# Layer norm's epsilon and wrap-around copy move from GpSimd to VectorE, the first q pieces are split for two token blocks, and two planner constants change

## The chip, the cores and the metric

One core of a Trainium2 chip runs the whole kernel. The metric is the device time in microseconds of one execution. Five engines work side by side, each through its own program in order: TensorE (PE: matmuls, and PEld: its weight loads), VectorE (DVE), ScalarE (ACT), GpSimd (POOL), and SyncE (SP), which here only issues DMA transfers. Engines wait for each other through semaphores.

## What is computed

One layer with two branches on the same normalised input: sliding-window attention with 32 heads of 18 and a gated feed-forward. Cut to what matters:

```python
xn = (x - mean(x)) / sqrt(var(x) + 1e-5)          # x: 2048 tokens x 576
q, k, v = split(xn @ wqkv)                        # wqkv: 576 x 1728
p = softmax(where(0 <= i - j < 256, q @ k.T * 18**-0.5, -1e9))
s = (p @ v).reshape(2048, 576) @ wo
h = sigmoid(xn @ w_gate) * (xn @ w_up)            # 576 x 4608 each
out = x + s * silu(h @ w_down)                    # 4608 x 576
```

## The kernel before

**Tiles and stages.** The 2048 tokens are four chunks of 512, a chunk four blocks of 128 tokens. Chunk c goes through layer norm (`build_ln`), the projections (`build_qkv`, 12 of them, q, k and v of each block), attention (`build_attn`), the output projection (`build_wo`), gate and up of the feed-forward with the down projection behind it (`build_ffn`). Gate and up fill TensorE; the scores and P*V of the same chunk are interleaved with them in small units.

**Layer norm of a block** (lines 424 to 441), in names used below: two statistics over half a row each, `bn1` and `bn2` (VectorE); the aggregate `ag` to mean and variance (VectorE); `ve`, the variance plus epsilon, one number per token (GpSimd, L431); `rstd`, that number to the power of -0.5 (GpSimd, L433); `apply`, subtract the mean and multiply by rstd over 576 columns (VectorE, L437) into a row of 640; and `wrap`, which fills columns 576 to 639 of that row with the normalised first 64 columns (GpSimd, L441: the same formula on 64 columns of x). The wrapped row serves the transposed layout: nine slices of 64 features, each present on both halves of the partitions.

**Into the transposed layout.** In chunk 0 TensorE transposes the row in nine pieces of 128 columns, the first four (`XT_CUT`) behind `apply` and the other five behind `wrap` (L462, `tr`); ScalarE copies each group out of the accumulator into `xn` (L472, `xe`). In chunks 1 to 3 two DMA transposes a block do that (`xt`), which wait for `apply` and `wrap`, and for the feed-forward of the chunk before to be done with `xn`.

**Projections.** `project` (L486) makes q, k or v of one block out of nine slices for two halves of the columns, 18 matmuls. For q of block 0 of chunk 0 alone they are two operations: the first four slices, which need only the first ScalarE copy and the first two of the four weight loads, and the rest. The order of the projections of chunk 0 is chosen by the planner; q and k of chunk 0 then go through DMA transposes (`qkt`) into `qkp`, from which the scores read.

**What sets the order.** The kernel is written as a list of operations with an engine, an estimated duration, dependencies and a priority. `schedule` plays them through: at each step an engine takes the operation with the smallest (earliest start + 40 ns x priority), the start being the planned time at which its dependencies are done, and for a DMA that plus a `slack`. The result is a fixed program for each engine; on the chip each operation waits on semaphores alone, so planned times decide the order and nothing else. In chunk 0 the layer norm of block i has the priority `LN_STEP * (i - 4)` on VectorE, TensorE and ScalarE, -12, -9, -6, -3; `ve` and `rstd` have 0. `XT0_SLACK` is the slack of `qkt` in chunk 0: so many ns after the planned landing the scores may be planned. Weights are issued on SP's queue, in the order of priorities: x, wqkv, then gate and up in groups of three tiles of 128 columns.

Of the kernel before, what the change touches and what calls it, by code (L numbers as in the profile page):

```python
# [5 lines left out]
ALU = mybir.AluOpType  # L6

S = 2048
D = 576
# [15 lines left out]
DP = NKT * P  # L25
EPS = 1e-5
# [53 lines left out]
XT0_ISSUE_NS = 1500.0  # L80
OC_SLACK = 3000.0
LATE_SLACK = 5000.0
LN_STEP = 3
EZ = 2
XT_CUT = 4
SC_GATE = 0
PV_PRIO = (2, 3)
PC_PRIO = 1
# [11 lines left out]
X0_FACTOR = 1.7  # L100
XT_BYTES = 1.2
XT0_BYTES = 1.5
XT0_SLACK = 1200.0
W0_FACTOR = 1.5
DMA_LAT_NS = 1600.0
DMA_BYTES_PER_NS = 320.0
# [2 lines left out]
def mm_ns(n):  # L109
    return max(28.0, n / 2.4 + 2.5)  # L110


def act_ns(n):
    return n / 1.2 + 80.0
# [72 lines left out]
class Builder:  # L187
# [16 lines left out]
    def op(self, eng, occ, fn, name, deps=(), prio=3, **kw):  # L204
        o = Op(eng, occ, fn, name, deps, prio, **kw)
        o.cidx = len(self.ops)
        self.ops.append(o)
        return o
# [199 lines left out]
    def build_ln(self, c):  # L408
        op = self.op
        pr = 0 if c == 0 else 2  # L410
        _, dxn = self.r_xn.take()
        self.op_xn = [[] for _ in range(QPC)]
        for i in range(QPC):
            st = c * QPC + i
            if c == 0:
                pr = LN_STEP * (i - QPC)
            ring, buf = (self.r_xf, self.xf) if c == 0 and i >= NXR else (self.r_xr, self.xr)
            sx, dx = ring.take()
            xs = buf[:, sx, :]
            o_x = self.dma(xs, self.x[st * P:(st + 1) * P, :], (X0_FACTOR if c == 0 and i > 1 else 1.0) * P * D * 2, f"x{st}",  # L420
                           ("x", i if c == 0 else sx), deps=dx + ([self.op_f1[(c - 1, 6 + 3 * i)]] if c > 0 else []),
                           prio=X_PRIO[i] if c == 0 else 4, slack=X0_SLACK if c == 0 else LATE_SLACK)
            sb_, db_ = self.r_bn.take()
            b1 = op("DVE", 360, lambda e, sb_=sb_, xs=xs: e.bn_stats(self.bnst[:, sb_, 0, :], xs[:, 0:288]),  # L424
                    f"bn1:{st}", deps=[o_x] + db_, prio=pr)
            b2 = op("DVE", 360, lambda e, sb_=sb_, xs=xs: e.bn_stats(self.bnst[:, sb_, 1, :], xs[:, 288:576]),
                    f"bn2:{st}", deps=[o_x] + db_, prio=pr)
            ag = op("DVE", 120, lambda e, st=st, sb_=sb_: e.bn_aggr(self.mv[:, st, :], self.bnst[:, sb_, :, :]),
                    f"ag:{st}", deps=[b1, b2], prio=pr)
            self.r_bn.release(sb_, ag)  # L430
            ve = op("POOL", 100, lambda e, st=st: e.tensor_scalar(self.veps[:, st, :], self.mv[:, st, 1:2], EPS,  # L431
                                                                 None, ALU.add), f"ve:{st}", deps=[ag], prio=0)
            rs = op("POOL", 560, lambda e, st=st: e.tensor_tensor(self.rstd[:, st, :], self.veps[:, st, :],  # L433
                                                                 self.neghalf[:, :], ALU.pow),
                    f"rstd:{st}", deps=[ve, self.op_negh], prio=0)
            sr, dr = self.r_xnr.take()
            ap = op("DVE", 350, lambda e, st=st, xs=xs, sr=sr: e.tensor_scalar(  # L437
                self.xnr[:, sr, 0:D], xs, self.mv[:, st, 0:1], self.rstd[:, st, :],
                ALU.subtract, ALU.mult), f"apply:{st}", deps=[rs, ag] + dr, prio=pr)
            ring.release(sx, ap)  # L440
            wr = op("POOL", 200, lambda e, st=st, xs=xs, sr=sr: e.tensor_scalar(  # L441
                self.xnr[:, sr, D:DP], xs[:, 0:64], self.mv[:, st, 0:1], self.rstd[:, st, :],
                ALU.subtract, ALU.mult), f"wrap:{st}", deps=[rs, ag] + dr, prio=pr)
            ring.release(sx, wr)
            tok = slice(i * P, (i + 1) * P)
            if c > 0:
                for k, (i0, i1, col) in enumerate(((0, NKT, 0), (NKT, NC, 64))):
                    o = self.dma(self.xn[:, i0:i1, tok], self.xnr[:, sr, col:col + (i1 - i0) * P],
                                 XT_BYTES * (i1 - i0) * P * P * 2, f"xt:{st}.{k}", ("xt", i, k), deps=[wr, ap] + dxn,
                                 prio=-2, issue=XT_ISSUE_NS, transpose=True)  # L450
                    self.r_xnr.release(sr, o)
                    self.op_xn[i].append(o)
                continue
            cols = [k * P for k in range(NKT)] + [64 + k * P for k in range(NC - NKT)]
            for i0, i1, dep in ((0, XT_CUT, ap), (XT_CUT, NC, wr)):
                n = i1 - i0
                ps = Psum((4,), (5,), (6,), (7,), (0,), (1,), (2,), (3,))

                def f_tr(e, sr=sr, ps=ps, i0=i0, i1=i1):
                    b = ps.banks[0] * 1024  # L460
                    for k, col in enumerate(cols[i0:i1]):
                        r = e.transpose(self.psb[:, b + k * P:b + (k + 1) * P], self.xnr[:, sr, col:col + P],  # L462
                                        self.op_[:, NOT - 1, 0:P])
                    return r
                tr = self.pe(n * 58, f_tr, f"tr:{st}", deps=[dep, ap, self.op_ident] + dxn, prio=pr, psum=[ps])
                tr.keep = False
                self.r_xnr.release(sr, tr)

                def f_xe(e, i=i, ps=ps, i0=i0, n=n):
                    b = ps.banks[0] * 1024  # L470
                    src = self.psb[:, b:b + n * P].rearrange("p (k c) -> p k c", k=n)
                    return e.activation(self.xn[:, i0:i0 + n, i * P:(i + 1) * P], src, ACTF.Copy)  # L472
                self.op_xn[i].append(self.rd("ACT", act_ns(n * P), f_xe, f"xe:{st}", deps=[tr], prio=pr, psum=[ps]))
        self.all_xn = [o for l in self.op_xn for o in l]
        if c == 0:
            for o in self.op_ez[EZ:]:
                o.odeps += self.op_xn[-1]

    def project(self, c, i, j, name, deps, after=None):
        ps = Psum((4, 5), (6, 7), (0, 1), (2, 3))  # L480

        def f(e, k0, k1):
            for k in range(k0, k1):
                for hf in range(2):
                    r0 = 64 * hf
                    r = e.matmul(self.bank(ps, HV, hf), self.xn[r0:r0 + 64, k, i * P:(i + 1) * P],  # L486
                                 self.wqkv_sb[r0:r0 + 64, j, k, :], start=(k == 0), stop=(k == NC - 1),
                                 tile_position=(r0, 0))
            return r
        odeps = [after]  # L490
        k0 = 0
        if c == 0 and i == 0 and j == 0:
            k0 = XT_CUT
            odeps = [self.pe(k0 * mm_ns(HV), lambda e: f(e, 0, k0), name + ":0",
                             deps=self.op_xn[i][:1] + self.op_wqkv[j][:2] + deps, prio=1, psum=[ps], mode="r64")]
        o = self.pe((NC - k0) * mm_ns(HV), lambda e: f(e, k0, NC), name, deps=self.op_xn[i] + self.op_wqkv[j] + deps,
                    prio=1, psum=[] if k0 else [ps], mode="r64", odeps=odeps)
        if k0:
            ps.users.append(o)
        self.r_xn.release(0, o)  # L500
        return o, ps
# [20 lines left out]
    def build_qk(self, c, i, j, old):  # L522
# [21 lines left out]
        if c == 0:  # L544
            if j == 0:
# [3 lines left out]
            dm = self.dma(dst, both, 2 * XT0_BYTES * 8 * P * P * 2, f"qkt:{c}:{i}", ("qk", i), deps=[ev, self.op_qe[i]] + old,  # L549
                          prio=0, issue=XT0_ISSUE_NS, transpose=True, slack=XT0_SLACK)  # L550
            if i > 0:
# [285 lines left out]
    def build_ffn(self, c):  # L837
# [67 lines left out]
        for n0, n1 in zip(cuts, cuts[1:]):  # L905
# [69 lines left out]
            prev = o  # L975
            if n0 == SC_GATE and c > 0:
                for l in self.op_sc[c]:
# [339 lines left out]
```

## Time and profile before

| | us |
|---|---|
| median of 3 runs (565.69 to 565.73) | 565.73 |
| the profiled execution | 565.84 |
| its span, first to last instruction | 564.1 |
| TensorE busy in it | 555.5 |
| VectorE busy | 302.9 |
| ScalarE busy | 279.3 |
| GpSimd busy | 44.0 |

A row of the timeline gives the start and the length in us, the engine, the line of the kernel, the operation, what is written and read, the shapes and how many instructions were merged; in brackets stand the idle time ahead of it and what ended that. A row of the stretches gives the length of the stretch and then, for PE, PEld, DVE, ACT and POOL, the busy time and the number of instructions, then TensorE's granted clock, the share of DMA time (it can pass 1, as transfers overlap) and GB/s. A row of the chain of waits gives start, length and what the end of the program hung on at that time. A row of DMA issues gives how many, how large, and the us from the issue to the landing. Matmuls are pipelined, and the end of a matmul row is modelled.

### The profile page before, as it was taken

How to read it: one execution, taken by the hardware profiler on the slowest of the kernel's cores; microseconds unless marked ns; L12 is line 12 of the kernel's file. 1: busy time of each engine (PE TensorE's matmuls, PEld its weight loads, DVE VectorE, ACT ScalarE, POOL GpSimd, SP SyncE). 2: the span in 40 equal slices, each digit the busy share in tenths (PEclk: the TensorE clock that was granted, in tenths of full speed). 3: DMA queues.
4: the chain of work that ended last, by engine and by line, in shares of the span. 5: the costliest groups of instructions: out<-in, count | busy, mean ns of one | idle time of the engine just before them, and what ended most of it. 6: DMA issues, size and time to landing. Idle time of an engine off the chain costs nothing.

```text
span 564.1 us, 17922 instructions
## 1 busy us (share of the span) xinstructions
PE 555.5 (98%) x7831; PEld 287.7 (51%) x7854; DVE 302.9 (54%) x624; ACT 279.3 (50%) x382; POOL 44.0 (8%) x87
## 2 busy tenths in 40 slices
PE   7999999999999999999999999999999999999997
PEld 4644444458544444456754444445665444444554
DVE  5135988722136886772214778666211576776312
ACT  7437777414155847721407575580230856856021
POOL 5000201110000210020000021002000000000100
PEclk9999999999999999999999999999999999999999
DMA  8999978929945766225893566604589365650010
GB/s 200 223 204 181 215 184 218 239 62 135 186 96 132 163 143 158 60 52 87 145 217 73 136 153 136 154 27 68 94 152 189 76 128 128 148 130 24 20 43 23
DMA packets 125900, 73.31 MB, mean 130 GB/s; under 512 B 54654, under 2 KB 125310, under 8 KB 125822
## 3 DMA queue, kind: packets, MB, share of 16 engines
q1 hardware_dynamic: 125822, 72.16, 61.3%
q8 instruction: 62, 1.02, 0.8%
q14 instruction: 16, 0.13, 0.1%
HBM read 55.48 MB, written 2.36 MB: 103 GB/s over the span
## 4 chain that ended last, share of the span: by engine, by line
PE 96%; POOL 1%; issue 1%; DVE 1%; ACT 0%; DMA 0%; DVEq 0%; POOLq 0%
PE ps L874 51%; PE ps L1001 23%; PE ps L486 9%; PE ps L632 5%; PE ps L702 3%; PE ps L795 3%; PE ps L1032 2%; POOL rstd L433 0%; POOL xnr L441 0%; DMA xr<-in_A_x_dram 0%; ACT expr L650 0%; POOL veps L431 0%; PE ps L462 0%; DVE hT L892 0%; DVE bnst L424 0%
## 5 line engine op out<-in xcount | busy, mean ns | idle before, releaser
L874 PE MATMUL ps<-xn,wgs 64*128 64x512 bf16 x2522 | 290.0, 377 | 0.2 <-DVE hT L892 0.2
L874 PEld LDWEIGHTS ps<-xn,wgs 64*128 64x128 bf16 x2522 | 116.4, 94 | 139.8 <-issue 10.3
L650 ACT ACTIVATE expr<-ps 128x1024 bf16<-128x1024 f32 x152 | 149.3, 1023 | 23.5 <-PE ps L632 23.5
L1001 PE MATMUL ps<-wd_sb,hT 128*128 128x64 bf16 (+1 forms) x1057 | 131.1, 284 | 2.1 <-issue 1.3
L888 ACT ACTIVATE tring<-ps 128x512 bf16<-128x512 f32 x144 | 86.2, 599 | 77.5 <-PE ps L874 59.4
L892 DVE SCALAR_TENSOR_TENSOR hT<-tring,ps 128x512 bf16<-128x512 bf16 x144 | 98.3, 683 | 46.3 <-ACT tring L888 23.9
L1001 PEld LDWEIGHTS ps<-wd_sb,hT 128*128 128x128 bf16 x1080 | 68.2, 98 | 65.0 <-issue 1.4
L668 DVE TENSOR_TENSOR expr<-expr,m 128x512 bf16<-128x512 bf16 (+2 forms) x152 | 58.1, 412 | 37.9 <-ACT expr L650 36.8
L1063 ACT ACTIVATE thf<-ps 128x576 bf16<-128x576 f32 (+2 forms) x17 | 10.6, 623 | 133.0 <-PE ps L1001 125.4
L1065 DVE SCALAR_TENSOR_TENSOR thf<-thf,ps 128x576 bf16<-128x576 bf16 (+2 forms) x17 | 12.2, 719 | 109.0 <-ACT thf L1063 108.9
L486 PE MATMUL ps<-wqkv_sb,xn 64*128 64x288 bf16 x864 | 55.0, 283 | 0.0
L486 PEld LDWEIGHTS ps<-wqkv_sb,xn 64*128 64x128 bf16 x864 | 42.7, 94 | 10.4 <-issue 0.5
L632 PEld LDWEIGHTS ps<-qkp 18*64 18x64 bf16 x1472 | 16.4, 103 | 32.8 <-ACT expr L650 18.2
L632 PE MATMUL ps<-qkp 18*64 18x320 bf16 (+4 forms) x1472 | 32.4, 259 | 0.0
L679 POOL COPY qkp<-qkp 128x256 bf16<-128x256 bf16 x24 | 9.8, 409 | 247.4 <-PE ps L632 247.4
L759 DVE STREAM_TRANSPOSE op__63<-pk 128x512 bf16<-128x512 bf16 x32 | 22.5, 702 | 0.3
L702 PEld LDWEIGHTS ps<-expr,vau 64*32 64x32 bf16 x1440 | 17.9, 92 | 7.2 <-issue 5.1
L702 PE MATMUL ps<-expr,vau 64*32 64x320 bf16 (+5 forms) x1440 | 20.7, 253 | 0.0
L1067 DVE TENSOR_TENSOR thf<-thf,sat 128x576 bf16<-128x576 bf16 (+2 forms) x17 | 7.5, 440 | 23.2 <-ACT sat L819 22.9
L795 PE MATMUL ps<-wo_sb,oT 64*128 64x288 bf16 x288 | 18.8, 283 | 0.2 <-issue 0.2
L319 POOL MEMSET pk<- 128x2048 bf16 x4 | 7.2, 1805 | 147.8 <-DVE op__63 L759 147.8
L541 ACT ACTIVATE pk<-ps 128x576 bf16<-128x576 f32 x13 | 8.5, 652 | 15.9 <-PE ps L486 13.6
(63 smaller groups left out, 246.5 us busy)
## 6 DMA issues: line engine op xcount, KB each, us to landing
wgs<-in_B_w_gate_dram SPq DMA_DIRECT2D x47, 240.0 KB, 3.8
wgs<-in_B_w_up_dram SPq DMA_DIRECT2D x47, 240.0 KB, 4.8
wgs<-in_B_w_up_dram SPq DMA_DIRECT2D x47, 192.0 KB, 4.1
wgs<-in_B_w_gate_dram SPq DMA_DIRECT2D x47, 192.0 KB, 4.4
wd_sb<-in_B_w_down_dram SPq DMA_DIRECT2D x9, 576.0 KB, 6.8
xf<-in_A_x_dram SPq DMA_DIRECT2D x18, 144.0 KB, 2.6
out_dram<-xf SPq DMA_DIRECT2D x15, 144.0 KB, 2.0
xr<-in_A_x_dram SPq DMA_DIRECT2D x14, 144.0 KB, 4.9
```

Source lines behind the costliest of these rows:

```text
L486: r = e.matmul(self.bank(ps, HV, hf), self.xn[r0:r0 + 64, k, i * P:(i + 1) * P], self.wqkv_sb[r0:r0 + 64, j, k, :], start=(k == 0), stop=( ...
L632: r = e.matmul(self.ps[64 * half:64 * half + 64, b:b + n * 64], self.qkp[r0:r0 + DH, hg, k0:k0 + 64], self.qkp[r0:r0 + DH, hg, q0 * 64:(q0 ...
L650: return e.activation(self.expr[:, es, 2 * pr:2 * pr + 2, :], src, ACTF.Exp, scale=SM_SCALE)
L668: return e.tensor_tensor(ap, ap, m, ALU.mult)
L702: r = e.matmul(self.ps[32 * j:32 * j + 32, b + q0 * 64:b + (q0 + n) * 64], vf[:, v0:v0 + 32], self.expr[p0:p0 + 64, es, j, pos * 64:(pos + ...
L759: t2 = self.op("DVE", dve_ns(CH), lambda e, on=on: e.transpose(self.op_[:, hg % NOT, :], on.rearrange("p g d -> p (g d)")), f"t2:{c}:{hg}" ...
L795: r = e.matmul(self.bank(ps2[w], HV, n), self.oT[r0:r0 + 64, kt, qi * P:(qi + 1) * P], self.wo_sb[r0:r0 + 64, kt, n * HV:(n + 1) * HV], st ...
L874: return e.matmul(self.bank((pg, pu)[gu][ft]), w, self.xn[r0:r0 + 64, i, :], start=first, stop=last, tile_position=(r0, 0))
L888: return e.activation(self.tring[:, st_, :], self.bank(ps), ACTF.Tanh, scale=0.5)
L892: return e.scalar_tensor_tensor(self.hT[:, ft, :], self.tring[:, st_, :], 1.0, self.bank(ps), ALU.add, ALU.mult)
L1001: r = e.matmul(self.ps[:, b + n0:b + n1], lhsT, self.wd_sb[:, q, fl, n0:n1], start=(ft == 0), stop=(ft == NFT - 1))
L1065: q1 = self.rd("DVE", dve_ns(n), lambda e: e.scalar_tensor_tensor(t, t, 1.0, yap(), ALU.add, ALU.mult), f"fq1:{sb}:{c0}", deps=[th], prio= ...
```

## The change

`ve` moves to VectorE with the block's priority, `rstd` gets the block's priority too, in all chunks. `wrap` becomes a copy on VectorE of the first 64 normalised columns, and so waits for `apply`; it no longer reads x. A step of priority between the blocks of chunk 0 is 1 and no longer 3. The first four slices of q are an operation of their own for blocks 0 and 1. The planned slack of the chunk-0 transposes that the scores read is 2000 ns and no longer 1200. The second group of transposes waits for `wrap` alone, which waits for `apply`.

```diff
-LN_STEP = 3
+LN_STEP = 1
 EZ = 2
 XT_CUT = 4
+Q_SPLIT = (0, 1)
...
-XT0_SLACK = 1200.0
+XT0_SLACK = 2000.0
...
-            ve = op("POOL", 100, lambda e, st=st: e.tensor_scalar(self.veps[:, st, :], self.mv[:, st, 1:2], EPS,
-                                                                 None, ALU.add), f"ve:{st}", deps=[ag], prio=0)
+            ve = op("DVE", 100, lambda e, st=st: e.tensor_scalar(self.veps[:, st, :], self.mv[:, st, 1:2], EPS,
+                                                                 None, ALU.add), f"ve:{st}", deps=[ag], prio=pr)
             rs = op("POOL", 560, lambda e, st=st: e.tensor_tensor(self.rstd[:, st, :], self.veps[:, st, :],
                                                                  self.neghalf[:, :], ALU.pow),
-                    f"rstd:{st}", deps=[ve, self.op_negh], prio=0)
+                    f"rstd:{st}", deps=[ve, self.op_negh], prio=pr)
...
-            wr = op("POOL", 200, lambda e, st=st, xs=xs, sr=sr: e.tensor_scalar(
-                self.xnr[:, sr, D:DP], xs[:, 0:64], self.mv[:, st, 0:1], self.rstd[:, st, :],
-                ALU.subtract, ALU.mult), f"wrap:{st}", deps=[rs, ag] + dr, prio=pr)
-            ring.release(sx, wr)
+            wr = op("DVE", 100, lambda e, sr=sr: e.tensor_copy(self.xnr[:, sr, D:DP], self.xnr[:, sr, 0:64]),
+                    f"wrap:{st}", deps=[ap], prio=pr)
...
-                tr = self.pe(n * 58, f_tr, f"tr:{st}", deps=[dep, ap, self.op_ident] + dxn, prio=pr, psum=[ps])
+                tr = self.pe(n * 58, f_tr, f"tr:{st}", deps=[dep, self.op_ident] + dxn, prio=pr, psum=[ps])
...
-        if c == 0 and i == 0 and j == 0:
+        if c == 0 and i in Q_SPLIT and j == 0:
```

## The prediction

> **What bounds the kernel now.** I read the page first, then busy time by stretch, then the chain of waits of the opening, then the opening's timeline engine by engine.
>
> ```profile
> span 564.1 us, 17922 instructions
> PE 555.5 (98%) x7831; PEld 287.7 (51%) x7854; DVE 302.9 (54%) x624; ACT 279.3 (50%) x382; POOL 44.0 (8%) x87
> 12.00:24.00 12.00, 12.00 (x200) 9.48 (x196) 2.27 (x3) 5.99 (x9) 0.00 (x0) 1.00 1.13 224
> 44.00:106.00 62.00, 61.80 (x1070) 28.49 (x1068) 48.05 (x111) 48.08 (x66) 8.03 (x18) 1.00 0.89 215
> ```
>
> TensorE (second number of a stretch, after its length) is full from 12 us on, at granted clock 1.00. So whatever the edits do to other engines after 12 us is hidden unless it stops TensorE, and a gain can only come from the first 12 us. There the chain of waits reads:
>
> ```profile
> 5.20 0.74 POOL xnr L441
> 5.94 0.21 POOL veps L431
> 6.22 0.58 POOL rstd L433
> 6.90 0.73 POOL xnr L441
> ...
> 11.68 12.23 PE ps L486 x198
> 23.92 20.29 PE ps L874 x188
> ```
>
> One block of the layer norm goes round every 1.70 us (5.20 to 6.90), all on POOL: wrap 0.74, epsilon 0.21, rstd 0.58 and gaps. From 11.68 TensorE runs through. What it does before that:
>
> ```profile
> 3.42 0.44 DVE L426 BATCH_NORM_STATS2 bnst<-xr 128x6 f32<-128x288 bf16 x1
> 3.90 0.21 DVE L428 BATCH_NORM_AGGREGATE mv<-bnst 128x2 f32<-128x12 f32 x1
> 4.02 0.41 DVE L424 BATCH_NORM_STATS2 bnst<-xr 128x6 f32<-128x288 bf16 x1
> 4.35 0.44 DVE L426 BATCH_NORM_STATS2 bnst<-xr 128x6 f32<-128x288 bf16 x1
> 5.13 0.43 DVE L437 TENSOR_SCALAR xnr<-xr,mv,rstd 128x576 bf16<-128x576 bf16 x1
> 5.67 0.60 PEld L462 LDWEIGHTS ps<-op__63,xnr 128*128 128x128 bf16 x9 [0.61 <-POOL rstd L433]
> 5.70 0.75 PE L462 MATMUL ps<-op__63,xnr 128*128 128x128 bf16 x9
> 6.12 1.19 ACT L472 ACTIVATE xn<-ps 128x512 bf16<-128x512 bf16 x2 [1.08 <-PE ps L462]
> 7.39 0.75 PE L462 MATMUL ps<-op__63,xnr 128*128 128x128 bf16 x9 [0.95 <-DVE xnr L437]
> 8.07 0.67 PE L486 MATMUL ps<-wqkv_sb,xn 64*128 64x288 bf16 x8
> 9.08 0.83 PE L462 MATMUL ps<-op__63,xnr 128*128 128x128 bf16 x9 [0.34 <-DVE xnr L437]
> 9.28 0.17 DVE L348 COPY m<-m 64x64 bf16<-64x64 bf16 x1
> 9.85 0.79 PE L486 MATMUL ps<-wqkv_sb,xn 64*128 64x288 bf16 x10
> 10.85 0.83 PE L462 MATMUL ps<-op__63,xnr 128*128 128x128 bf16 x9 [0.22 <-DVE xnr L437]
> ```
>
> The idle marked on the matmul rows is 0.95+0.34+0.22 = 1.5 us, but those rows end with a modelled tail. By starts there is more. Nine transposes take 0.60 (the weight loads); a projection matmul takes 12.23/198 = 0.062, so the pieces of 8 and 10 take 0.50 and 0.62. Then TensorE is idle from 6.30 to 7.39 (1.09), 8.57 to 9.08 (0.51) and 10.47 to 10.85 (0.38), and inside the last two groups of transposes 0.17 each (0.77 to the next start against 0.60): **2.3 us**. From the first transpose to the end of the projections are 23.92-5.70 = 18.2 us, of which 15.9 are work.
>
> **The change part by part.** *POOL loses epsilon and wrap.* Its round falls to rstd alone, 0.58 plus some 0.1, far below 1.70.
>
> *VectorE gains both.* No epsilon on VectorE is in the trace: from below 0.12 (from the small aggregate at 3.90 to the start behind it at 4.02), from above 0.21 (the same operation on POOL). I take 0.2, the aggregate (0.21) being nearest in shape and engine; as it is pipelined it occupies about 0.1. The wrap copy of 128x64: from below 0.12, from above the 0.74 on POOL; I take 0.17, the 64x64 copy. Both come out as one block on VectorE of two statistics at 0.35 (4.02 to 4.35), aggregate 0.12, epsilon 0.1, apply 0.35 to 0.43, wrap 0.1 to 0.17: 1.4 to 1.5 us, so VectorE becomes the pacemaker, at a shorter round.
>
> *LN_STEP 1.* A priority step is worth 40 ns in the planner, so a block is preferred to the next by 40 ns and no longer 120. The planner's rule is used here for the order alone. After bn2 of block 0 its aggregate is ready 105 ns later than bn1 of block 1 can start; 120 outweighed that, 40 doesn't. The new order on VectorE is bn1:0, bn2:0, bn1:1, ag:0, bn2:1, ve:0, ag:1, bn1:2, ve:1, bn2:2, ap:0, ag:2, wrap:0, ap:1, ve:2, wrap:1, bn1:3, bn2:3, ap:2, ag:3, wrap:2, ve:3, and the mask copies ahead of ap:3. With the rows' start-to-start times: bn1:0 3.04, bn2:0 3.42, bn1:1 3.80, ag:0 4.17, bn2:1 4.29, ve:0 4.64 to 4.84, rstd (0.1 behind, as the transposes' loads at 5.67 behind the apply's end at 5.56) 4.94 to 5.51, and behind ag:1, bn1:2, ve:1 and bn2:2 ap:0 starts at 5.70 instead of 5.13 and ends at 6.13. **The first transpose is late by 0.54**: 6.24 instead of 5.70. That is the loss in this change.
>
> *From there TensorE should hardly wait.* The order on it by the same rule: tr0, tr1, first piece of q0, tr2, first piece of q1 (the new Q_SPLIT), rest of q0, tr3, rest of q1, q2, v0. tr0 6.24 to 6.84 (wrap:0 needed at 6.51, there at 6.45); tr1 to 7.44 (ap:1 ends at 6.71); first q0 piece from 7.54 (a switch costs 0.1, as 7.97 to 8.07) to 8.04; ap:2 follows its rstd (6.91 to 7.48) at 7.58 and ends at 8.01, so tr2 starts at 8.12: idle 0.08. The first q1 piece at 8.82 needs the third ACT copy, which runs from 7.85 to 8.44 (0.595 each from 6.66 on). It fills what was idle before tr3, and Q_SPLIT costs no instruction: the same 18 matmuls in two pieces. The rest of q0 at 9.32; ap:3 ends at 9.54, before 9.94. Idle left: 0.1 to 0.2. **End of the projections: 6.24+15.9+0.15 = 22.3, against 23.92: 1.6 us earlier.** From both ends: by the marked idle alone 1.5-0.54 = 1.0; with all 2.3 gone and ap:0 at rstd's end, 5.55, 2.3-0.4 = 1.9.
>
> *Is what comes next there in time?* The loads do not move with TensorE: the queue issues them back to back.
>
> ```profile
> 2.67 8.04 SPq L227 DMA_DIRECT2D wqkv_sb<-in_A_wqkv_dram  x12
> wqkv_sb<-in_A_wqkv_dram SPq DMA_DIRECT2D x1, 180.0 KB, 4.2
> wqkv_sb<-in_A_wqkv_dram SPq DMA_DIRECT2D x1, 180.0 KB, 4.5
> 35.75 2.26 SPq L226 DMA_TRANSPOSE qkp<-expr  x1
> qkp<-expr SPq DMA_TRANSPOSE x1, 6.3
> 44.13 0.43 PE L632 MATMUL ps<-qkp 18*64 18x64 bf16 x24
> ```
>
> The fourth weight load (issued at 2.67+3*0.67 = 4.68) lands at 8.9, needed at 9.32; the eighth (7.36) at 11.9, and v0 starts at 12.2 behind q2. The last transpose for the scores lands at 42.05. The scores start at 44.13 now; 1.6 earlier would leave half a microsecond, and XT0_SLACK plans them 0.8 later, one or two pieces of the feed-forward of three pairs (0.65). So they come at 43.2 to 43.8, and the edit costs nothing as long as those pieces fill TensorE; without them it would be up to 1.3. These covers of 0.3 us and more all hold at 1.6.
>
> *Later chunks.* Eight small VectorE operations a chunk, some 1.2 us, lie beside a VectorE that has 14 us free in 62; TensorE does not wait for them. The dropped second dependency of the transpose is implied by the wrap.
>
> [...] The apply now runs while POOL computes the next rstd. Rows of a later chunk, and of another:
>
> ```profile
> 250.72 1.80 POOL L319 MEMSET pk<- 128x2048 bf16 x1 [1.72 <-DVE op__63 L759]
> 250.59 2.10 DVE L437 TENSOR_SCALAR xnr<-xr,mv,rstd 128x576 bf16<-128x576 bf16 x1
> 387.00 0.73 POOL L441 TENSOR_SCALAR xnr<-xr,mv,rstd 128x64 bf16<-128x64 bf16 x1 [8.63 <-DMA xn<-xnr]
> 387.30 0.35 DVE L437 TENSOR_SCALAR xnr<-xr,mv,rstd 128x576 bf16<-128x576 bf16 x1
> ```
>
> Beside a POOL memset the apply takes 2.10 us and ends 0.17 after it; beside a wrap it takes 0.35. If rstd blocks as the memset does, ap:0 (5.70) waits for rstd:1 (5.57 to 6.14) and ends at 6.31: 0.18 later than I have it, a gain of 1.4. If it blocks as the wrap does, nothing. I take nothing, since rstd touches one column. [...]
>
> **The rivals.** *rstd blocks the apply*, as just worked out: 564.3. For it: the 2.10 row. Against: the 0.35 row.
>
> *VectorE becomes the bound and holds TensorE as POOL did.* If each new operation costs a full dependent round, 0.48 as from bn2 at 3.42 to its aggregate at 3.90, five of them lie ahead of ap:2, each 0.3 above my price: tr2 at 9.6, 1.4 more idle, a gain of 0.2: 565.5. Against it: epsilon and wrap of one block stand behind other work in the order, so the wait is mostly over.
>
> *Attention of chunk 0 runs past its feed-forward: slower.* The place is the end of the stage (two rows of the chain for a round, then the timeline):
>
> ```profile
> 51.16 2.48 PE ps L874 x22
> 53.64 0.35 PE ps L632 x16
> ```
>
> ```profile
> 104.06 1.11 PE L702 MATMUL ps<-expr,vau 64*32 64x320 bf16 x72
> 105.10 1.04 PE L874 MATMUL ps<-xn,wgs 64*128 64x512 bf16 x8
> 106.30 3.87 PE L1001 MATMUL ps<-wd_sb,hT 128*128 128x64 bf16 x31 [0.16 <-issue]
> ```
>
> Behind the last P*V lie 1.0 us of feed-forward and, before the next step that must follow P*V, 8 down-projection matmuls (3.87/31 = 0.125 each): 2.0 us of cover. Scores that start 0.7 to 1.3 later against the feed-forward use up part of it. If the new plan also loses one round of scores (22 matmuls and 16 scores, 2.48+0.35 = 2.84), TensorE waits 1.3+2.84-2.0 = 2.1 and the change ends 0.5 slower: 566.3. It turns from a lateness of 3.6 us on. For it: the shared accumulators bind each round. Against: between 44 and 106 TensorE lacks 0.2 us in all, and the plan behind q1 stays in step with the old one, since the edits move its times there hardly at all.
>
> **How the numbers follow.** The profiled execution took 565.84 for a span of 564.1, so 1.74 lie around it; the median of the runs shown is 565.73, 0.11 below. 564.1-1.6+1.74-0.11 = **564.1**. Chances: forecast 0.60, rstd blocks 0.12, VectorE the bound 0.13, attention past the end 0.15. What a measurement of this kernel can tell from no change is about 0.2%, or 1.13 us, so faster means below 564.6. The forecast's own range is 563.8 (gain 1.9) to 564.7 (gain 1.0), nearly all of it faster; with the port case, less what falls above 564.6, 0.68. The VectorE case and the mild part of the last give 0.18 for within, the rest 0.14 slower. The range runs from 563.6, a little below the largest gain as the 0.2 us that TensorE lacks of 62 between 44 and 106 may come back too, to 565.5, the VectorE case, and leaves out the last.
>
> **What would show it.** VectorE's first apply at about 5.7 and the first transpose at about 6.2; between it and the first gate/up matmul at about 22.2 no idle of TensorE above 0.2; POOL with rstd alone in the chunk-0 layer norm; scores first at 43.2 to 43.8 without a wait; TensorE full from 7.5 us to the end. It is wrong if tr2 or tr3 still wait for an apply by half a microsecond, if q1's second piece waits for weights, or if a wait appears before the P*V near 103 us or the down projection behind it.

## The result and the profile after

| | before | changed |
|---|---|---|
| median of 15 runs, us | 565.70 | 564.47 |
| lowest to highest | 565.49 to 565.88 | 564.28 to 565.02 |
| the profiled execution | 565.84 | 564.39 |
| its span | 564.1 | 562.2 |
| around the span | 1.74 | 2.19 |
| VectorE busy | 302.9 | 305.4 |
| GpSimd busy | 44.0 | 29.3 |

The changed kernel takes 0.9979 of the time before, with a 95% interval of 0.9971 to 0.9987: 1.23 us less. Two executions among those of the later kernels, one of the kernel before with the new step and one of the changed kernel run again, took 2009 and 2458 us; the ratios leave them out, and the medians in the table below would be 0.03 and 0.01 lower without them. The forecast was 564.1, its range 563.6 to 565.5. The span fell by 1.9, more than forecast; 0.45 of that came back as time outside the span.

From the page of the changed kernel, its first line and that of a queue that carries instructions (packets, MB, share):

```profile
span 562.2 us, 17899 instructions
...
q14 instruction: 14, 0.11, 0.1%
```

Its chain of waits, from the first epsilon on:

```profile
4.61 0.05 DVE veps L432
4.66 0.19 DVE mv L429
...
5.18 0.05 DVE veps L432
...
5.60 0.33 DVE xnr L438
...
6.08 1.17 PE ps L461 x18
7.24 0.66 PE ps L485 x8
7.90 0.61 PE ps L461 x9
8.51 1.21 PE ps L485 x18
9.72 0.61 PE ps L461 x9
10.33 11.74 PE ps L485 x190
22.07 21.37 PE ps L873 x198
43.44 0.36 PE ps L631 x16
```

GpSimd has left the chain. Until 5.9 us it runs through VectorE without a gap, and from 6.08 each TensorE piece begins where the one before ends. The pieces are those of the forecast: 18 transposes, 8 matmuls of q0, nine transposes, 18 matmuls, nine transposes, 190 matmuls. The timeline of the same stretch, with the stretch of 2 us in which VectorE has the most to do:

```profile
4.53 0.14 DVE L432 TENSOR_SCALAR veps<-mv 128x1 f32<-128x1 f32 x1
4.75 1.21 POOL L434 TENSOR_TENSOR rstd<-veps,neghalf 128x1 f32<-128x1 f32 x2 [1.84 <-DVE veps L432]
5.51 0.41 DVE L438 TENSOR_SCALAR xnr<-xr,mv,rstd 128x576 bf16<-128x576 bf16 x1
5.96 0.18 DVE L442 COPY xnr<-xnr 128x64 bf16<-128x64 bf16 x1
```

```profile
6.00:8.00 2.00, 1.93 (x29) 1.56 (x30) 2.00 (x11) 1.50 (x3) 0.55 (x1) 1.00 0.92 236
```

Between 6 and 8 us VectorE is busy for 2.00 of 2.00 and TensorE for 1.93: VectorE is full, and TensorE does not have to wait for it. Later, the changed kernel at the step that must follow the last P*V of chunk 0:

```profile
104.18 17.59 PE L1000 MATMUL ps<-wd_sb,hT 128*128 128x64 bf16 x141 [0.16 <-issue]
```

It stood at 106.30 before: 2.12 earlier, 0.27 more than the 1.85 won by the end of the projections. The chain of the kernel before shows where these 0.27 lay, and a row of its timeline how long the wait was:

```profile
47.42 0.69 DVE hT L892
48.12 0.14 issue
48.25 2.55 PE ps L874 x22
```

```profile
48.25 1.24 PE L874 MATMUL ps<-xn,wgs 64*128 64x512 bf16 x9 [0.20 <-DVE hT L892]
```

TensorE was idle for 0.20 until VectorE had written hT, and the 22 matmuls behind took 2.55 where 2.48 is usual.

In the changed kernel TensorE has 198 and no longer 188 gate and up matmuls ahead of the first scores (last two rows of its opening chain), and the wait is gone. A new one stands in chunk 2. The chain of before, then of the changed kernel:

```profile
337.86 7.23 PE ps L874 x66
345.09 0.35 PE ps L632 x16
```

```profile
335.76 5.30 PE ps L873 x48
...
342.39 0.61 DVE pk L722
342.99 0.14 issue
343.13 0.42 PE ps L631 x16
```

The 66 matmuls used to run into the scores (337.86+7.23 = 345.09). Now the same 66 would end at 335.76+7.23 = 342.99; the scores start at 343.13, behind three VectorE operations that follow the end of the first 48 at 341.06, of which the last, L722, reads an accumulator out, and take 0.42 instead of 0.35: 0.21 lost.

The account of the profiled execution: projections end 1.85 earlier (22.07 against 23.92), 0.27 from the wait near 48 us, less some 0.22 in chunk 2, makes the 1.9 of the spans; less 0.45 around the span, 1.45, which is 565.84-564.39.

### The profile page after: what moved, and what is told of

Read it like the earlier page. It is cut to its first block, busy times and chain, and to the rows that moved or that the text cites. A ratio compares the mean times of both kernels' runs of the same rounds, so it can differ in the third digit from the quotient of the medians.

```text
span 562.2 us, 17899 instructions
## 1 busy us (share of the span) xinstructions
PE 555.1 (99%) x7831; PEld 287.6 (51%) x7854; DVE 305.4 (54%) x656; ACT 279.1 (50%) x382; POOL 29.3 (5%) x55
## 4 chain that ended last, share of the span: by engine, by line
PE 98%; DVE 1%; issue 0%; DMA 0%; ACT 0%
PE ps L873 51%; PE ps L1000 23%; PE ps L485 10%; PE ps L631 5%; PE ps L701 3%; PE ps L794 3%; PE ps L1031 2%; PE ps L461 0%; DMA xr<-in_A_x_dram 0%; DVE bnst L425 0%; DVE bnst L427 0%; DVE hT L891 0%; DVE op__63 L758 0%; DVE pk L722 0%; DVE mv L429 0%
## 5 line engine op out<-in xcount | busy, mean ns | idle before, releaser
L540 ACT ACTIVATE pk<-ps 128x576 bf16<-128x576 f32 x13 | 8.5, 652 | 15.9 <-PE ps L485 13.6
L794 PEld LDWEIGHTS ps<-wo_sb,oT 64*128 64x128 bf16 x288 | 14.4, 94 | 3.6 <-issue 0.7
```

What stands on the lines that cost most here:

```text
L794: r = e.matmul(self.bank(ps2[w], HV, n), self.oT[r0:r0 + 64, kt, qi * P:(qi + 1) * P], self.wo_sb[r0:r0 + 64, kt, n * HV:(n + 1) * HV], st ...
```

## The experiments

Times are medians, each beside the kernel before on the same chip (565.67 to 565.70), in three groups; the changed kernel was run again in the last. "Around the span" is the median over the runs of time less span; for the kernel before it was 1.74 to 1.75 in all three groups.

| kernel | us | median span | around | end of projections |
|---|---|---|---|---|
| before | 565.70 | 563.9 | 1.74 | 23.92 |
| changed | 564.47 | 562.3 | 2.19 | 22.07 |
| changed, again | 564.59 | 562.4 | 2.22 | 22.18 |
| changed, step 3 | 564.74 | 562.5 | 2.20 | 22.50 |
| before, step 1 | 566.74 | 565.0 | 1.74 | 24.74 |
| no second q split | 564.54 | 562.3 | 2.23 | 22.39 |
| slack 1200 | 564.81 | 562.6 | 2.21 | 22.47 |
| VectorE only in chunk 0 | 564.28 | 562.5 | 1.76 | 22.64 |
| epsilon on GpSimd | 564.24 | 562.5 | 1.75 | 22.80 |
| wrap on GpSimd | 564.17 | 562.4 | 1.77 | 22.61 |
| wrap on GpSimd, again | 564.23 | 562.5 | 1.76 | 22.74 |
| block 0 preferred | 564.98 | 562.8 | 2.20 | 22.76 |
| small GpSimd operations added | 564.37 | 562.6 | 1.75 | 22.25 |
| aggregate first | 564.43 | 562.7 | 1.75 | 22.61 |

The last column is of one profile each, and the speed of the first transposes varies in it (last section).

### The step between the blocks, with and without the relief of GpSimd

The changed kernel with the old step:

```diff
-LN_STEP = 1
+LN_STEP = 3
```

> The changed kernel with LN_STEP back at 3, all else as changed. Theory (step 1 interleaves the blocks, so VectorE's dependent operations hide behind the next block's statistics; its price is a first transpose 0.4 to 0.5 us later): with step 3 the first transpose comes at about 5.6 instead of 6.08, but each block waits out its own chain, about 1.65 us a block, the last transposes start near 10.4 instead of 9.65, the projections end 0.7 us later than in the changed kernel, and the time is about 565.2. Rival (the late first transpose is a real loss, the later blocks would be in time anyway): 0.4 us faster than the changed kernel, 564.1.

564.74 us, ratio 0.9983 (0.9975 to 0.9992). Its timeline:

```profile
5.53 0.66 PE L461 MATMUL ps<-op__63,xnr 128*128 128x128 bf16 x9
7.05 0.68 PE L461 MATMUL ps<-op__63,xnr 128*128 128x128 bf16 x9 [0.86 <-DVE xnr L438]
```

The first transpose comes 0.55 earlier than in the changed kernel, as the prediction had it (0.54); but the second block then makes TensorE wait 0.86, and the projections end 0.43 later: the theory's direction, at a good half of its 0.7, and the time lies halfway between theory and rival. Against the changed kernel it is 0.27 and 0.15 slower (its two medians); the intervals overlap. The other way round, the kernel before with the new step alone:

```diff
-LN_STEP = 3
+LN_STEP = 1
```

> The kernel before with the step between token blocks at 1 and nothing else. Theory A (the step frees little by itself, because GpSimd still does epsilon, power and wrap of each block, 1.7 us a block, and that round paces the blocks; the first transpose comes later because block 1's statistics stand ahead of block 0's): TensorE still waits 0.4 to 0.7 us ahead of block 2's or block 3's transposes, projections end at 23.4 to 23.9, 565.2 to 565.8 us. Theory B (the order of the blocks is what gave the gain, the engine of epsilon and wrap does not matter, as the two kernels with only one of them moved came out alike): projections end at 22.3 to 22.8, 564.3 to 564.7 us.

566.74 us, ratio 1.0019 (1.0010 to 1.0028): slower than before by 1.05, which neither theory had. Its chain:

```profile
5.33 0.74 POOL xnr L441
...
7.03 0.74 POOL xnr L441
...
11.45 0.44 PE ps L462 x5
11.89 12.85 PE ps L486 x208
```

GpSimd's round is still 1.70 us (5.33 to 7.03) and starts 0.13 later than before, so the last transposes end 0.21 later (11.89 against 11.68). And the planner, which now thinks the blocks close together, writes the last transposes ahead of the rest of q0: behind them stand 208 matmuls and no longer 198, ten matmuls of 0.062 that used to fill a wait. 0.21+0.62 = 0.83, and the projections end at 24.74 instead of 23.92. That is the profiled executions, which differ by 0.73 in time; what the medians differ by more is not explained. By the medians, then, the step alone costs 1.05 us, the relief without the step (with the split and the slack) brings 0.96, and the whole change 1.1 to 1.2. So the step does harm where GpSimd sets the pace and none where VectorE does; that it gains some 0.2 there is likely from the projections' end, but not clear of the noise in the times. The step with the split and the slack, and no relief, was not run.

### Which of the two moved operations does it

Epsilon back on GpSimd, at its old priority, and in the second kernel the wrap-around back instead:

```diff
-            ve = op("DVE", 100, lambda e, st=st: e.tensor_scalar(self.veps[:, st, :], self.mv[:, st, 1:2], EPS,
-                                                                 None, ALU.add), f"ve:{st}", deps=[ag], prio=pr)
+            ve = op("POOL", 100, lambda e, st=st: e.tensor_scalar(self.veps[:, st, :], self.mv[:, st, 1:2], EPS,
+                                                                 None, ALU.add), f"ve:{st}", deps=[ag], prio=0)
...
-                    f"rstd:{st}", deps=[ve, self.op_negh], prio=pr)
+                    f"rstd:{st}", deps=[ve, self.op_negh], prio=0)
```

> The changed kernel with epsilon back on GpSimd in all chunks, wrap still on VectorE. Theory (of the 1.70 us round on GpSimd the wrap's 0.74 was what had to go; rstd and epsilon alone, 0.57+0.23 and gaps, are a round of 0.95, shorter than VectorE's 1.4): the projections end within 0.2 us of the changed kernel's 22.07, time 564.3 to 564.6. Rival (epsilon's place on the chain between aggregate and rstd counts for each block): 0.2 to 0.4 us a block, time 565.0 or more.

```diff
-            wr = op("DVE", 100, lambda e, sr=sr: e.tensor_copy(self.xnr[:, sr, D:DP], self.xnr[:, sr, 0:64]),
-                    f"wrap:{st}", deps=[ap], prio=pr)
+            wr = op("POOL", 200, lambda e, st=st, xs=xs, sr=sr: e.tensor_scalar(
+                self.xnr[:, sr, D:DP], xs[:, 0:64], self.mv[:, st, 0:1], self.rstd[:, st, :],
+                ALU.subtract, ALU.mult), f"wrap:{st}", deps=[rs, ag] + dr, prio=pr)
```

> The changed kernel with the wrap back on GpSimd in all chunks, epsilon still on VectorE. Theory: rstd and wrap make a round of 1.4 us on GpSimd and each wrap stands ahead of the next rstd; the transposes of blocks 2 and 3 wait, the projections end 0.6 to 0.9 us later, time 565.2. Rival (any shortening of GpSimd's round below VectorE's is enough): within 0.1 us of the changed kernel, 564.5.

564.24 us (0.9974, 0.9964 to 0.9984) and 564.17 us (0.9973, 0.9963 to 0.9983): either move alone, beside the step, the split and the slack, gives the whole gain in time, and the loss expected from a wrap on GpSimd did not come. In the span they give 0.1 to 0.2 less than the whole change, and in the profiles the projections end at 22.80 and 22.61, later than the 0.2 that the first theory allowed: with epsilon on GpSimd the chain runs through its powers down to 7.27, and with the wrap there it runs through a wrap (6.06 to 6.62) ahead of 14 of the first transposes (6.67). The timeline of GpSimd with the wrap back on it:

```profile
4.85 1.21 POOL L434 TENSOR_TENSOR rstd<-veps,neghalf 128x1 f32<-128x1 f32 x2 [1.93 <-DVE veps L432]
5.96 1.15 POOL L442 TENSOR_SCALAR xnr<-xr,mv,rstd 128x64 bf16<-128x64 bf16 x2
```

The powers of blocks 0 and 1 now follow each other (x2) ahead of both wraps. Before, a wrap and an epsilon stood between them, 0.74+0.21 and gaps. In this order no power of the first two blocks stands behind a wrap. That of block 2 does (7.06), and when this kernel was run again (below), VectorE's apply waited 0.42 for it (7.66); the time, 564.17, does not show it. In this kernel epsilon has left GpSimd and the power has a new priority; which of the two made the order was not tested, and neither was the power's priority by itself. With epsilon on GpSimd and the wrap on VectorE, GpSimd's round falls from 1.70 to 0.85 and 0.96 us (epsilons at 4.48, 5.33 and 6.29). Its chain still runs through GpSimd from 4.48 to 7.27, with VectorE's apply of block 2 behind it at 7.37: here GpSimd has not given up the pace, only quickened it.

Run once more beside the unedited changed kernel:

> The changed kernel with the wrap-around back on GpSimd, a second time, beside the changed kernel on the same chip. Theory A (it is really 0.3 us below the changed kernel, through the 0.45 us around the span less 0.15 inside it): 564.1 to 564.3 us, 0.2 to 0.4 below the changed kernel of this group. Theory B (the difference was one of chips and sessions): within 0.1 us of the changed kernel.

> The changed kernel once more, unedited, beside the other three of this group, so that they stand against it on the same chip. Every theory expects its span at 562.1 to 562.8 us, 2.2 us around the span, and 564.5 us, with a spread of some 0.5 us from run to run that the first transposes' pace makes.

564.23 (0.9973, 0.9963 to 0.9984) against 564.59 (0.9980, 0.9971 to 0.9989) on the same chip: 0.36 less, as theory A had it, 0.46 less around the span and about 0.1 more inside. The intervals overlap, and the kernels with epsilon on GpSimd (564.24) and with VectorE only in chunk 0 (564.28) are not to be told from it: the whole change is not the best of these.

### The time around the span, and chunk 2

The new operations on VectorE in chunk 0 only, the old code in the others:

```diff
-            ve = op("DVE", 100, lambda e, st=st: e.tensor_scalar(self.veps[:, st, :], self.mv[:, st, 1:2], EPS,
-                                                                 None, ALU.add), f"ve:{st}", deps=[ag], prio=pr)
+            ve = op("DVE" if c == 0 else "POOL", 100, lambda e, st=st: e.tensor_scalar(self.veps[:, st, :], self.mv[:, st, 1:2], EPS,
+                                                                 None, ALU.add), f"ve:{st}", deps=[ag], prio=pr if c == 0 else 0)
...
-            wr = op("DVE", 100, lambda e, sr=sr: e.tensor_copy(self.xnr[:, sr, D:DP], self.xnr[:, sr, 0:64]),
-                    f"wrap:{st}", deps=[ap], prio=pr)
+            if c == 0:
+                wr = op("DVE", 100, lambda e, sr=sr: e.tensor_copy(self.xnr[:, sr, D:DP], self.xnr[:, sr, 0:64]),
+                        f"wrap:{st}", deps=[ap], prio=pr)
+            else:
+                wr = op("POOL", 200, lambda e, st=st, xs=xs, sr=sr: e.tensor_scalar(
+                    self.xnr[:, sr, D:DP], xs[:, 0:64], self.mv[:, st, 0:1], self.rstd[:, st, :],
+                    ALU.subtract, ALU.mult), f"wrap:{st}", deps=[rs, ag] + dr, prio=pr)
```

> The changed kernel with epsilon and wrap on VectorE for chunk 0 alone; chunks 1 to 3 have them on GpSimd, as before the change. Theory (the 0.23 us that the changed kernel loses again in chunk 2, near 341 us, come from the small operations that VectorE carries there): that wait goes, the span falls from 562.2 to 562.0 and the time by 0.2, to 564.2. It would also tell whether the 0.4 us by which the time outside the span grew (1.74 before, 2.2 after) goes with GpSimd's share of the program: then the time falls to 563.8. Rival (the wait in chunk 2 comes from another order of the plan): the span stays at 562.2.

564.28 us, ratio 0.9976 (0.9967 to 0.9986). Its chain in chunk 2 is whole again:

```profile
336.17 7.23 PE ps L879 x66
343.40 0.35 PE ps L637 x16
```

From the end of the projections to the last stage (L1031, in this kernel L1037) it takes 527.80 us, the changed kernel 528.18 and 528.02, the one before 528.20. Around the span lie 1.76 again. So both parts of the theory are seen, 0.2 to 0.4 behind the projections and 0.45 around the span, and yet the time is 564.28 and not 563.8, and the median span rose by 0.2: in the profile the projections end 0.5 later, after a late landing of x (last section) and slow first transposes. What the time around the span depends on, the next run isolates: the changed kernel with 24 tiny GpSimd operations in chunks 1 to 3, whose results nobody uses.

```diff
+            if c > 0:
+                for d in range(2):
+                    self.dum = op("POOL", 100, lambda e: e.tensor_scalar(
+                        self.neghalf[:, 1:2], self.neghalf[:, 0:1], EPS, None, ALU.add), f"dum:{st}:{d}",
+                        deps=[ag, self.op_negh, getattr(self, "dum", None)], prio=0)
```

> The changed kernel plus 24 one-column GpSimd instructions in chunks 1 to 3 that nothing waits for (they write a spare column). Outside the span lie 1.74 us in the kernel before, 2.2 in the changed one and in the runs with its layer norm in all chunks, 1.8 where chunks 1 to 3 keep their GpSimd instructions. Theory (what lies outside the span hangs on the number of GpSimd's instructions): 1.8 outside, time 564.1. Rival (it hangs on something else that chunks 1 to 3 changed): 2.2 outside, time 564.5, the same as the changed kernel.

564.37 us (0.9978, 0.9968 to 0.9987): the time around the span falls from 2.2 to 1.75 though work was added, and the median span rises by 0.2 to 0.3. Its page has one more packet in the queue that carries instructions (first line); the kernel before had two more (second):

```profile
q14 instruction: 15, 0.12, 0.1%
q14 instruction: 16, 0.13, 0.1%
```

All kernels of the table with 14 such packets have 2.19 to 2.23 around the span, all with 15 or 16 have 1.74 to 1.77; the former have 55 GpSimd instructions on their pages, the latter 71 or more. So the 0.45 are shown to hang on how many instructions GpSimd's program has, not on what they do in the span; by what way is not shown. Why the span gives back most of it in this run stays open. The opening rows show no shift with the packets: GpSimd's memset of `vau` starts at 1.73 in the changed kernel (14) and with VectorE only in chunk 0 (15). From the end of the projections to the last stage this kernel takes 528.27.

The wait in chunk 2 is in the changed kernel's two profiles, in this one and without the second q split. It is absent where epsilon or the wrap is on GpSimd in chunk 2, but also with step 3, with block 0 preferred and with slack 1200, in which VectorE has all the same operations there: these three have 188 gate and up matmuls ahead of the first scores, those with the wait 198. So it comes with both together, the operations on VectorE and the order that the planner wrote, and is not simply VectorE having too much to do.

### The second q split

```diff
-Q_SPLIT = (0, 1)
+Q_SPLIT = (0,)
```

> The changed kernel with the first q piece split for block 0 alone. Theory (the split fills TensorE between the transposes of blocks 2 and 3): without it TensorE is idle there for about 0.5 us, 8 matmuls of 0.062, and the time is 565.0. Rival (the planner finds other work for the place, or the weights' landing at 8.9 sets it anyway): within 0.1 us of the changed kernel.

564.54 us, ratio 0.9981 (0.9972 to 0.9989), not to be told from the changed kernel. The chain:

```profile
8.62 0.14 issue
8.76 1.89 PE ps L485 x28
10.65 0.61 PE ps L461 x9
```

TensorE waits 0.15 for the third and fourth weights (in the chain a transfer from 4.80 to 8.62), which the first four slices of q1 would have covered, then runs the rest of q0 and the whole of q1 ahead of the last transposes. From the first transpose to the end of the projections are 16.23 us (6.16 to 22.39) against 15.99: the split is worth 0.24 in the profile. The larger loss expected without it did not come: as the rival had it, the planner filled the place with other work, the whole q1.

### The planned slack

```diff
-XT0_SLACK = 2000.0
+XT0_SLACK = 1200.0
```

> The changed kernel with XT0_SLACK back at 1200. Theory (the later scores are what removed the wait of 0.2 us at 48 us, as the feed-forward's start moved by 1.85 us but its end by 2.12): the scores come one or two pieces (0.65 us each) earlier, at 42.8 or 42.1, the end of chunk 0's feed-forward comes 0.2 to 0.3 us later than in the changed kernel, 564.7. Rival 1 (the slack does nothing for the time): the same as changed, with the scores earlier and no wait. Rival 2 (the scores then catch the DMA transposes in flight): TensorE waits up to 0.5 us or more at the first scores, 565.0 or above.

564.81 us, ratio 0.9983 (0.9974 to 0.9992). The wait of the kernel before is back:

```profile
42.76 0.36 PE ps L631 x16
43.12 3.13 PE ps L873 x28
46.25 0.35 PE ps L631 x16
46.60 0.13 issue
```

The scores at 42.76 do not wait for their transposes either, so the later plan was not needed for them. It gains by another way: 28 matmuls between the first two rounds of scores leave TensorE waiting for VectorE's hT (it ends at 46.59, the matmul behind it starts at 46.74), 22 do not. From the end of the projections to those of chunk 1 this kernel takes 99.90 us (122.37 less 22.47), the changed one 99.70 (121.77 less 22.07) and the one before 99.97. The wait is in the kernels with step 3 and with block 0 preferred too, at the slack of 2000: the slack is one way to the better order, not its cause alone.

### Putting block 0 first in the new kernel

Two edits for the 0.54 us by which the first transpose came later. Block 0 preferred by two priority steps more:

```diff
-                pr = LN_STEP * (i - QPC)
+                pr = LN_STEP * (i - QPC) - (2 if i == 0 else 0)
```

> The changed kernel with the priority of block 0 two steps lower still (-6, -3, -2, -1), so that its aggregate and epsilon go ahead of block 1's first statistics. Two theories on the spread of the changed kernel (564.28 to 565.02). Theory A (in the changed order block 1's statistics stand ahead of block 0's aggregate, so the landing of the second x transfer, 3.5 in some executions and 3.9 in others, is on the chain): here that landing has half a microsecond of cover, the slow end of the spread goes and all runs lie within 0.3 us. Rival B (the spread comes from elsewhere, as from TensorE's pace in the first transposes): the spread stays at 0.7. For the median: the first transpose comes at 5.5 instead of 6.1, but the second block's later, so that TensorE waits 0.5 to 1.0 there; the time lies between 564.2 and 564.7.

564.98 us, ratio 0.9988 (0.9980 to 0.9997): slower than the changed kernel by 0.4 to 0.5, above the 564.2 to 564.7 expected, and closer from run to run (564.86 to 565.07). Its chain runs through VectorE down to 8.54, leaves 198 matmuls behind the last transposes where the changed kernel has 190, and has the wait near 47 us again. The narrow spread is what theory A expected, but does not show it: here TensorE's slow first transposes (last section) are off the chain too, and the kernels with epsilon or the wrap on GpSimd, in which block 1's statistics stand first as in the changed kernel, also lie within 0.3 and 0.4. What makes the spread stays open. And, with the new operations on VectorE in chunk 0 only, the aggregate of block 0 alone ahead of the first statistics of block 1:

```diff
-                    f"ag:{st}", deps=[b1, b2], prio=pr)
+                    f"ag:{st}", deps=[b1, b2], prio=pr - 2 if st == 0 else pr)
```

> Epsilon and wrap on VectorE in chunk 0 only, and block 0's aggregate put ahead of block 1's first statistics. Theory A (the landing of the second x transfer stands in the chain in the changed order, because block 1's statistics were put ahead of block 0's aggregate; with the aggregate first, GpSimd's power of block 0 starts 0.3 to 0.5 us earlier and a late landing of block 1 is hidden): the first transpose starts at 5.6 to 5.9 us whatever block 1's landing is, the projections end at 21.8 to 22.1, the downstream stays as without the chunk-2 wait, 563.8 to 564.1 us with 1.75 around the span. Theory B (what is saved at the head is waited for by block 1 or by TensorE's first slow products): projections still end at 22.1 to 22.6, 564.2 to 564.4 us.

564.43 us, ratio 0.9977 (0.9968 to 0.9986): theory B, a hair above its range; the kernel that it was made from took 564.28. Its timeline of TensorE and the end of its opening chain:

```profile
5.86 0.66 PE L467 MATMUL ps<-op__63,xnr 128*128 128x128 bf16 x9 [0.16 <-DVE veps L432]
7.04 0.68 PE L467 MATMUL ps<-op__63,xnr 128*128 128x128 bf16 x9 [0.52 <-DVE xnr L438]
```

```profile
9.12 0.35 DVE xnr L438
...
9.51 0.74 PE ps L467 x9
10.26 12.36 PE ps L491 x200
22.61 21.37 PE ps L879 x198
```

The first transposes come 0.22 earlier than in the changed kernel, 0.43 earlier than in the kernel that this one was made from, and TensorE waits 0.52 for block 1. The chain runs through VectorE down to the last block's apply: VectorE is the pacemaker here, and 200 matmuls instead of 190 are left behind the last transposes. An earlier start of block 0 is worth nothing while the other blocks come at VectorE's round.

## Why the prediction was right, and where not

**GpSimd's round as the bound, VectorE as the next pacemaker: right.** GpSimd is out of the chain, the order on VectorE is the one written out, and TensorE runs through from the first transpose. That the step without the relief leaves GpSimd's round of 1.70 and the waits in place, and the relief without the step a wait of 0.86, is shown by the two runs on the step.

**"The first transpose is late by 0.54": right in kind, 0.16 too much.** It came at 6.08 and not 6.24, since epsilon occupies VectorE for 0.05 (4.61 to 4.66) where 0.1 was taken, twice, and the first statistics began a little earlier (3.00 against 3.04). That the same edit's lateness is 0.55 is shown by the step-3 run.

**"End of the projections 22.3, 1.6 us earlier": 22.07, 1.85 earlier.** Of the 0.23, 0.16 are the transpose. From there on it took 15.99 where the sum had 16.05: the idle of 0.15 in it is not there, and the work took 0.09 more than 15.9. The unknown price of the wrap copy, 0.17 from the 64x64 copy, came out as 0.18.

**rstd blocking the apply, the port case of the chances: refuted.** The powers run from 4.75 to 5.96, the apply from 5.51 for 0.41: it is not held. Longer is rather the power: the one beside that apply (5.31) takes 0.65, those beside none (4.75 and 6.62) 0.56 and 0.55. Nor was the apply held by a wrap on GpSimd before: 0.43 from 5.13, beside the wrap of 0.74 from 5.20. Beside the memset the apply of chunk 1 takes 2.10 again (109.29, the memset of 1.80 at 109.43). Why the memset goes with so long an apply and the power does not, by its one column as the forecast took it or otherwise, is not shown.

**"VectorE becomes the bound and holds TensorE": refuted for the kernel as it is, but near.** VectorE is full from 6 to 8 us (2.00 of 2.00); with the order tilted to block 0, TensorE waits 0.52.

**"Attention of chunk 0 runs past its feed-forward": refuted.** The step behind the last P*V comes 2.12 earlier, with the same 0.16 ahead of it. The scores started at 43.44, inside the 43.2 to 43.8 forecast. The 0.2 us that "may come back too" were 0.27.

**"Later chunks: TensorE does not wait for them": wrong by some 0.22**, the wait at 343 us.

**The time around the span, taken as fixed at 1.74: wrong by 0.45**, and the largest single miss. The four misses together, -0.25-0.27+0.22+0.45, are +0.15, just what parts the profiled execution (564.39) from the sum for it (564.1-1.6+1.74 = 564.24). That the number came out so near is thus partly luck: 0.52 of gain and 0.67 of loss were left out, and nearly cancel. The forecast is 0.37 below the median for 0.15 of this, 0.03 of rounding, and 0.19 because the profiled execution lies 0.08 below its kernel's median and the one before lay 0.11 above its own (565.73).

## What to carry to other kernels

An order and an engine move can have opposite signs alone and together: here the new step costs 1.05 us while GpSimd sets the pace and nothing once it is relieved, so test each of the four corners. When a pacemaker with two jobs per block is relieved, moving either job can be all of it (564.24 and 564.17 here, 564.47 with both); look then at which job stands ahead of the one that the next block waits for. Compare spans as well as times: the change that took instructions from GpSimd here moved the time around the span by 0.45, and the plan with the shifted opening brought a wait at 343 us.

## What the runs showed of the hardware

**Time outside the span went with the length of GpSimd's program, in a step.** With 14 packets in the instruction queue (55 GpSimd instructions) 2.2 us lie around the span, with 15 or 16 (71 or more) 1.75; 24 instructions more shortened it.

**TensorE's pace at the start varies, at a granted clock of 1.00.** Nine transposes take 0.61 in the changed kernel's chain at 7.90 and at 9.72. Ahead of them, from 1.52 us on, stand ten matmuls that only keep TensorE busy (`warm`, L364); they take 3.87 with step 3 and 4.45 in the kernels shown here. The timeline of the kernel with block 0 preferred, then the chain of the kernel with VectorE only in chunk 0, and a stretch of the latter's opening:

```profile
5.76 1.17 PE L461 MATMUL ps<-op__63,xnr 128*128 128x128 bf16 x9
```

```profile
6.29 1.58 PE ps L467 x18
```

```profile
6.00:8.00 2.00, 1.71 (x22) 1.61 (x24) 2.00 (x10) 1.08 (x2) 0.73 (x2) 1.00 0.94 230
```

There nine transposes from 5.76 on take 1.17 (the wrap ahead of them ends at 5.61) where the first nine with step 3, which start at 5.53, take 0.66, and 18 from 6.29 take 0.41 more than 18 in the changed kernel (1.58 against 1.17). So the short time is there from 5.5 us on in one execution and not yet up to 6.8 in another, and by these two differences, 0.51 and 0.41, an end of the projections from a single profile is uncertain by some half a microsecond. What sets the moment is not shown: the granted clock reads 1.00 with step 3 (5.40 to 7.80), with block 0 preferred (6.00 to 7.20) and in the stretch above.

**The landing of the second x transfer can be on the path in the new order.** In the kernel with slack 1200 VectorE waits for it:

```profile
3.91 0.46 DVE L425 BATCH_NORM_STATS2 bnst<-xr 128x6 f32<-128x288 bf16 x1 [0.21 <-DMA xr<-in_A_x_dram]
```

In the changed kernel the same statistics start at 3.74 without a wait, with VectorE only in chunk 0 at 3.94 after a wait of 0.16. With the aggregate put first they start at 4.07, so that this wait would be covered, but that run showed that nothing is won by it.
